# Fourier layer and soft mixture of experts on one core: dummies bridging to the first px, and the combine products as pairs of 64-row products

## The chip, the cores and the metric

The kernel runs on one core of a Trainium2 chip. The metric is the time of one execution in microseconds (us), as the median of several timed runs. One execution was also recorded by the hardware profiler; all durations of single instructions come from that one. The engines are called as in the profile: PE is the matrix engine and PEld its weight load, DVE, ACT and POOL are the vector, scalar and general engines, and SP issues most transfers (DMAs). ACT can issue transfers too, on a queue of its own.

## The reference

Two layers follow each other. The first transforms `x` (8 x 2496 x 256) along the sequence, multiplies by a complex 256 x 256 matrix, adds a bias, shrinks by 0.01 and transforms back. The second is a soft mixture of experts with 8 experts of 4 slots each.

```python
X = np.fft.rfft(x, axis=1)
Yr = Xr @ w_r - Xi @ w_i + b_r
Yi = Xr @ w_i + Xi @ w_r + b_i
Yr = np.sign(Yr) * np.maximum(np.abs(Yr) - lam, 0.0)      # Yi likewise
y = np.fft.irfft(Yr + 1j * Yi, n=x.shape[1], axis=1)
...
logits = x @ phi                         # x: y as 19968 x 256, 32 slots
d = softmax(logits, axis=0)              # over the tokens
slot_out[e] = np.maximum((d.T @ x)[e] @ w1[e], 0.0) @ w2[e]
c = softmax(logits, axis=1)              # over the slots
return c @ slot_out                      # 19968 x 256
```

## The kernel before

The length 2496 is split as 39 x 64, and the transform runs in two stages. Stage a (`a_unit`) multiplies pieces of 117 tokens x 2 groups x 256 columns by the 39-point matrix `f1a`: a product `pa`, which ACT copies from PSUM into a tile `ast`. The `ast` tiles are written to DRAM (`adr`, and for a first part of batch 0 `ad`, `a_write`), and `load_ap` reads them back in another order as `ap`, 512 KB for each of the 40 steps (8 batches x 5 groups of frequencies). Stage f2 multiplies `ap` by the 64-point matrix `smov`: the product `px`. ACT and DVE split `px` into high and low parts (`xth`, `xtl`, `xsm`, `xsh`, `xsl`), `lin_k` and `lin_y` multiply by the weights (`pk`, `py`), and what follows makes logits and slot inputs. The first batch reads `x` through tiles `x0`, later ones through `xr`, of which three buffers exist.

The order of the work is written out by generators with due times: `step_to` puts a generator on a heap, `run_until` takes the earliest, and every engine executes its instructions in the order in which they were recorded. The numbers in `PLAN` are these due times. For the transfers of the beginning the order stands in `PLAN["seq"]`: the token `a0` is the load of `ap` for step 0, `r` the rest of a write of batch 0, `w4` a held write of batch 1, `x8` an `xr` load, `c`, `s` and `k` constants. `keep_warm` issues products of a tile of zeros whose result is not used (`wps`); they are called dummies here.

The first four stage-a pieces of batch 1 (`pa_0` to `pa_6` of that batch, `direct`) are calculated before the first `px`. The write of the piece with groups 4 to 7 is called adr4 below, from its tile `ast_4`; it uses a buffer of the tag `ap` (line 166), so that the third `ap` load can only start when that write has landed.

At the end `slot_out` is known (`po`). It is spread over partitions as high and low parts (`prep`, `rhs`), and the combine loop (line 1183) makes the output: 78 blocks of 128 token pairs, each with two groups of 256 columns. For each block `c_trans` has put transposed combine weights (`pc`, copied to `ct`) into SBUF: rows 0 to 63 belong to the first group, 64 to 127 to the second. `rhs[a]` is 128 x 512 with the slot outputs in rows 0 to 63 of its first half and rows 64 to 127 of its second; the rest is zero. ACT and DVE copy the blocks alternately from PSUM (`pq`, four buffers) to `ost` (nine buffers of 512 KB), and SP writes 512 KB for two blocks. Between the blocks stand the parts for the next batch: `c_prep` splits the combine weights (`chl`, first ACT, then DVE), and `c_trans` transposes them in three pieces. There are 9.75 blocks in a batch.

```python
        mm(
            out=pq,
            lhsT=cts[lo][:, j * TR - lo : j * TR - lo + TR],
            rhs=rhs[a].rearrange("p b d -> p (b d)"),
```

Of the kernel before, what the change touches and what calls it, by code (L numbers as in the profile page):

```python
# [11 lines left out]
F32 = mybir.dt.float32  # L12
# [17 lines left out]
KG = 4  # L30
# [20 lines left out]
def _constants():  # L51
# [95 lines left out]
    "f1": [1.5, 2.15],  # L147
    "kw": [[-40, 9]],
    "ap1": 1.85,
# [8 lines left out]
    "cl_": 'V',  # L158
    "a1": [-50, -49, -48, -47, 3.0, 4.0, 5.9, 6.9, 7.9, 8.9, 10.2],
    "e1": [0, 0, 0, 0, 0, 0, 0, 0, 1, 0, 1],  # L160
# [4 lines left out]
    "lsl": 'PPPPPPPPPPPPPPPPPPPPPPPV',  # L165
    "ast4": {(0, 18): "wr", (1, 0): "wr", (1, 4): "ap"},
    "nd": 4,
    "x1": {(1, 20): 3.5, (2, 0): 7.2},
    "ab1": [[0, 4], [4, 8], [8, 14], [14, 20], [20, 22]],
    "seq": ['a0', 'c', 'a1', 's', 'x8', 'r', 'r', 'r', 'r', 'w4', 'a2', 'x9', 'x10', 'w0', 'k'],  # L170
}
# [12 lines left out]
def fourier_soft_moe_kernel(ctx: ExitStack, tc: tile.TileContext, t: dict, out: bass.AP):  # L184
# [18 lines left out]
    def psum(tag, name):  # L203
        return pp.tile([128, 512], F32, tag=tag, name=name, bufs=psum_bufs[tag])
# [31 lines left out]
    def sp(**kw):  # L236
        tc.keep_in_program_order(nc.sync.dma_start(**kw))
# [16 lines left out]

    def load_x(i):
# [5 lines left out]
        sp(out=xr[:, :ng, :], in_=x[b, :, g : g + ng, :])  # L261
        xrs[(b, g)] = xr
# [63 lines left out]
    def a_unit(b, g, u):  # L326
# [26 lines left out]
        ast = asts[(b, gs[0])]  # L353
        po = psum(("pf", "pl", "pt")[i_ % 3] if first else "pf", f"pa{b}_{g}")
# [6 lines left out]
        yield tu + PLAN['ao']  # L361
        copy(
# [4 lines left out]
        if g + GP == gs[1]:  # L367
            if b == 1 and direct:
                held[gs[0]] = (ad[b], ast, *gs)
                return  # L370
            yield tu + 1.0
            if first:
                a_write(ad0, ast, *gs, 0, R * 4 * KG, q=aq)
                rest.append((ad[b], ast, *gs, R * 4 * KG, QA))
            else:
                a_write(ad[b], ast, *gs)
# [7 lines left out]
    def load_ap(b, grp):  # L384
        ap = wtile([128, KG, D], F32, "ap", f"ap{b}_{grp}")
        src = (ad0 if b == 0 and grp < 2 else ad[b]).rearrange("(k r) g d -> k (r g) d", r=R)
        src = src[grp * 2 * KG : (grp + 1) * 2 * KG, :N2]
        for c in range(2):
            sp(out=ap[c::2], in_=src[c * KG : (c + 1) * KG].rearrange("k n d -> n k d"))
        return ap  # L390

    def f2(s, c, t0):
        yield t0
        b, grp = steps[s]
        ap = aps[s]
        ps = psum("pf", f"px{b}_{grp}_{c}")
        for j in range(KG):
# [47 lines left out]
    def lin_k(s):  # L445
        t0 = 4 * s
        yield t0 + 0.35
        b, g = steps[s]
        pk = psum("pl", f"pk{b}_{g}")
        for c in range(2):  # L450
            lin_s(pk, c, xts[(s, c)])
        yield t0 + PLAN['ko']
        kss[s] = wtile([128, 2, 256], F32, "k1", f"k1{b}_{g}")
        A.copy(out=kss[s], in_=pk.rearrange("p (e x) -> p e x", e=2))

    def lin_y(s, e):
        b, grp = steps[s]
        end = s == ns - 1
        t0 = 4 * s + 1 + (PLAN["T_"]["ye"] if end else 1.35) * e
        yield t0  # L460
        py = psum("pl", f"py{b}_{grp}_{e}")
        lin(py, e, 0, xts[(s, 0)])
        if e == 1 and not end:
            t0 = 4 * s + 3
            yield t0
# [300 lines left out]
    sp(out=wri, in_=t["w"])  # L766
    load_x(7)
    for u, g in enumerate(range(0, G, GP)):
# [314 lines left out]

    rhs = []
    for a in range(2):
        rhs.append(wtile([128, 2, D], F32R, "p_sb", f"rhs{a}"))
        P.memset(rhs[a].bitcast(F32), 0.0)
    slz, hz = pools["slz"], pools["hz"]
# [76 lines left out]
    c_trans(0, 0, V)  # L1165
    for i, tag, dst in ((0, "ps", ((0, A), (1, A))), (1, "pl", ((0, V),)), (1, "pl", ((1, A),))):
        prep = psum(tag, f"prep{i}")
        mm(out=prep[:, :D], lhsT=dmr, rhs=so[i], start=True, stop=True)
        for a, eng in dst:
            r0 = slice(64 * a, 64 * a + 64)  # L1170
            copy(eng, rhs[i][r0, a, :], prep[r0, :D])
    c_trans(0, 4, V)
# [4 lines left out]
    for b in range(B - 1):  # L1177
# [3 lines left out]
        for i0, d, eng in ((0, 4, A), (4, 6, V), (8, 8, A)):  # L1181
            todo.setdefault(at0 + d, []).append((c_trans, b + 1, i0, eng))
    for j in range(NBLK):
        if j % 2 == 0:
            ost = hl_tile(f"ost{j}")
        pq = psum(("pf", "pl")[j % 2], f"pq{j}")
        lo = j * TR - j * TR % F
        for a in range(2):
# [9 lines left out]
        if j < 2 or j >= NBLK - 2:  # L1198
            sp(out=out[j // 2, :, half], in_=ost[:, half])
        elif j % 2:  # L1200
            sp(out=out[j // 2], in_=ost)
        run_until(1000 + 6 * j * TR / CB + 0.1)
        for fn, *args in todo.get(j, []):
            fn(*args)

# [57 lines left out]
```

## Time and profile before

| what | value |
|---|---|
| median of 3 runs | 567.42 us (566.44 to 567.63) |
| the profiled execution, own time | 563.34 us |
| its span in the profile | 561.5 us |
| PE busy | 521.4 us (93% of the span), 4354 matmul records |
| DVE, ACT, POOL busy | 422.0, 298.1, 281.1 us |
| moved by DMA | 121.44 MB, 216 GB/s over the span |
| chain that ended last, by engine | PE 70%, DVE 13%, DMA 10%, ACT 3% |

The profiled execution is 4.08 us shorter than the median of the timed ones. A time in the chain belongs to the instruction that the next one waited for; "idle before <-" names what ended an engine's wait. A product in plain f32 appears as two matmul records, one in fp32r as one. Matmul records overlap, so that the distance from start to start tells what one costs in a row of them.

### The profile page before, as it was taken

The numbers are of one execution on the slowest core, as the hardware profiler recorded it, in microseconds if no ns is written. First come the engines' busy times: TensorE is split into PE (matmuls) and PEld (weight loads), VectorE is DVE, ScalarE is ACT, GpSimd is POOL, SyncE is SP. The second block draws the span as 40 slices with busy tenths as digits, with TensorE's granted clock in tenths as the row PEclk, the third lists the DMA queues.
The fourth block names the chain that finished last, engine by engine and source line by source line (L and its number), as shares of the span: only waits on it lengthen the run. The fifth ranks groups of instructions, "written<-read, shape, count | busy, mean of one in ns | idle before, by whom it ended". The sixth has DMA issues, their size and how long they took to land.

```text
span 561.5 us, 11780 instructions
## 1 busy us (share of the span) xinstructions
PE 521.4 (93%) x4354; PEld 442.2 (79%) x4354; DVE 422.0 (75%) x837; ACT 298.1 (53%) x650; POOL 281.1 (50%) x258
## 2 busy tenths in 40 slices
PE   8669999999999999999999999999899979899794
PEld 4458999989898889889988898987687867367573
DVE  0347897799979897989789978986795764248783
ACT  4435555666566656665665666653433333147572
POOL 0037777766766576658655866684554402000100
PEclk9999999999999999999999999999999998999899
DMA  8788464756476637664757474766634378979898
GB/s 301 249 294 292 151 207 152 210 179 170 163 216 207 189 118 208 207 180 167 204 171 199 155 201 167 222 230 178 186 131 126 113 183 276 392 240 368 325 374 351
DMA packets 93684, 121.44 MB, mean 216 GB/s; under 512 B 46786, under 2 KB 68736, under 8 KB 93628
## 3 DMA queue, kind: packets, MB, share of 16 engines
q1 hardware_dynamic: 93372, 119.63, 65.4%
q10 hardware_dynamic: 256, 1.08, 0.5%
q8 instruction: 34, 0.56, 0.4%
q14 instruction: 22, 0.18, 0.1%
HBM read 69.87 MB, written 50.82 MB: 215 GB/s over the span
## 4 chain that ended last, share of the span: by engine, by line
PE 70%; DVE 13%; DMA 10%; ACT 3%; issue 2%; SPq 1%; ACTq 0%; DVEq 0%
PE py L243 16%; PE px L243 11%; PE pq L243 9%; PE pa L243 8%; PE pk L243 7%; PE pt L532 4%; PE pr L243 3%; DMA eb<-ed 2%; PE pc L1067 2%; DMA ad<-ast 2%; PE pe L243 2%; DMA ap<-adr 2%; DVE mx L180 1%; DVE clpL L180 1%; DVE xtl L180 1%
## 5 line engine op out<-in xcount | busy, mean ns | idle before, releaser
L180 POOL TENSOR_TENSOR rt<-ut,rt 128x512 f32<-128x512 f32 x79 | 111.7, 1414 | 24.4 <-DVE rt L180 18.4
L180 POOL TENSOR_TENSOR xsl<-xsm,xsh 128x256 fp32r<-128x256 f32 x77 | 59.3, 770 | 102.4 <-DVE xsh L180 71.0
L180 POOL TENSOR_TENSOR xl<-xr,xh 117x512 fp32r<-117x512 f32 x73 | 98.5, 1350 | 22.6 <-ACT xh L180 14.7
L243 PE MATMUL px<-smov,ap 128*128 128x128 f32 x640 | 85.6, 277 | 8.0 <-DMA ap<-adr 4.5
L243 PEld LDWEIGHTS px<-smov,ap 128*128 128x128 f32 x640 | 80.3, 193 | 13.7 <-issue 8.1
L180 ACT CAST xth<-px 128x512 fp32r<-128x512 f32 x80 | 46.8, 585 | 73.0 <-PE py L243 37.6
L180 ACT COPY ast<-pa 128x512 f32<-128x512 f32 x86 | 50.3, 587 | 64.5 <-PE pa L243 61.6
L180 DVE SCALAR_TENSOR_TENSOR ut<-py,pk,k 128x256 f32<-128x256 f32 x160 | 69.5, 475 | 15.0 <-PE py L243 13.1
L180 DVE TENSOR_TENSOR xtl<-px,xth 128x512 fp32r<-128x512 f32 x80 | 54.6, 682 | 26.8 <-ACT xsm L180 22.0
L243 PE MATMUL py<-xth,nwsh 128*128 128x256 f32 x160 | 53.5, 334 | 0.0
L180 DVE TENSOR_SCALAR rt<-ut 128x512 f32<-128x512 f32 x69 | 52.2, 756 | 0.5
L243 PE MATMUL pk<-xsh,w_rh 128*128 128x256 f32 x160 | 47.9, 300 | 2.0 <-DVE xsh L180 2.0
L180 ACT COPY T<-pt 128x512 f32<-128x512 f32 x70 | 42.1, 601 | 9.0 <-PE pt L532 7.3
L532 PE MATMUL pt<-pk,rt 128*128 128x128 f32 x320 | 45.9, 273 | 0.9 <-DVE dd L180 0.6
L243 PE MATMUL pk<-xsl,w_rh 128*128 128x256 f32 x160 | 45.1, 282 | 0.0
L243 PE MATMUL pk<-xsh,w_rl 128*128 128x256 f32 x160 | 44.9, 281 | 0.0
L243 PE MATMUL py<-xtl,nwsh 128*128 128x256 f32 x160 | 44.7, 279 | 0.0
L243 PE MATMUL py<-xtl,wdh 128*128 128x256 f32 x160 | 44.7, 279 | 0.0
L243 PE MATMUL py<-xth,wdl 128*128 128x256 f32 x160 | 44.7, 279 | 0.0
L243 PE MATMUL py<-xth,nwsl 128*128 128x256 f32 x160 | 44.7, 279 | 0.0
L243 PE MATMUL py<-xth,wdh 128*128 128x256 f32 x160 | 44.7, 279 | 0.0
L243 PE MATMUL pq<-rhs,ct 128*128 128x512 f32 x156 | 43.1, 415 | 0.3 <-DVE ost L180 0.3
(186 smaller groups left out, 1241.7 us busy)
## 6 DMA issues: line engine op xcount, KB each, us to landing
ap<-adr SPq DMA_DIRECT2D x76, 256.0 KB
out<-ost SPq DMA_DIRECT2D x37, 512.0 KB
xr<-in_x SPq DMA_DIRECT2D x35, 512.0 KB
adr<-ast SPq DMA_DIRECT2D x20, 768.0 KB
w<-in_moe_w SPq DMA_DIRECT2D x25, 512.0 KB
adr<-ast SPq DMA_DIRECT2D x8, 512.0 KB
w<-in_moe_w SPq DMA_DIRECT2D x14, 256.0 KB
x<-in_x SPq DMA_DIRECT2D x11, 256.0 KB
```

The lines of the kernel that those rows point to most:

```text
L180: return lambda *a, **k: self.tc.keep_in_program_order(f(*a, **k))
L243: tc.keep_in_program_order(nc.tensor.matmul(**kw))
L532: tc.keep_in_program_order(nc.tensor.transpose(out=out, in_=in_, identity=identity))
L1067: nc.tensor.transpose(out=pc[:, i * P1 : (i + 1) * P1], in_=chls[b][x][:, 2 * (r + i) : 2 * (r + i) + 2].rearrange("p g h s -> p (g h s)") ...
```

## The change

In the head of the kernel:

- The first `ap` buffers are allocated ahead of everything else, and adr4's tile comes from the three `ast` buffers instead of an `ap` buffer.
- The load of `xr_4` (512 KB) moves from SP, where it stood before the first `ap` load, to ACT's queue behind the last `ad` write.
- In `seq` the rest writes of batch 0 start earlier, and adr4 is no longer in it: it is written when its generator comes, behind the large constants (`k`).
- The dummies before the first `px` go from 9 to 18. `pa_4` and `pa_6` of batch 1, which stood before them, move behind the first `px`, between the parts of step 0.
- In step 0 DVE makes `xtl` last instead of first, and the first half of `py` comes between the two halves of `pk`.

In the combine loop:

- `rhs[a]` is 128 x 256 without zeros, so that POOL's two memsets and two of the four small copies go.
- A step of the loop takes two blocks. For each block and each of the two parts a there are two products of 64 rows and 256 columns, one per group, into two PSUM tiles. Before there was one product of 128 rows and 512 columns.
- ACT copies the first group of both blocks, DVE the second; every output write is 512 KB. `c_prep` and `c_trans` stand behind whole pairs of blocks.

```diff
-    "kw": [[-40, 9]],
+    "kw": [[-40, 18]],
...
-    "a1": [-50, -49, -48, -47, 3.0, 4.0, 5.9, 6.9, 7.9, 8.9, 10.2],
+    "a1": [-50, -49, -1.7, 0.42, 3.0, 4.0, 5.9, 6.9, 7.9, 8.9, 10.2],
...
-    "ast4": {(0, 18): "wr", (1, 0): "wr", (1, 4): "ap"},
+    "ast4": {(0, 18): "wr", (1, 0): "wr"},
...
-    "seq": ['a0', 'c', 'a1', 's', 'x8', 'r', 'r', 'r', 'r', 'w4', 'a2', 'x9', 'x10', 'w0', 'k'],
+    "seq": ['a0', 'r', 'a1', 'c', 's', 'r', 'x8', 'r', 'r', 'a2', 'x9', 'x10', 'w0', 'k'],
...
                 rest.append((ad[b], ast, *gs, R * 4 * KG, QA))
+                if gs[1] == G:
+                    load_x(7, aq)
...
-        V.tensor_tensor(out=xl, in0=pv, in1=xh.bitcast(F32), op=ALU.subtract)
+        if s:
+            V.tensor_tensor(out=xl, in0=pv, in1=xh.bitcast(F32), op=ALU.subtract)
...
+        if not s:
+            V.tensor_tensor(out=xl, in0=pv, in1=xh.bitcast(F32), op=ALU.subtract)
...
-    load_x(7)
+    ap_early = [wtile([128, KG, D], F32, "ap", f"ap0_{grp}") for grp in range(2)]
...
-        pq = psum(("pf", "pl")[j % 2], f"pq{j}")
-        lo = j * TR - j * TR % F
-        for a in range(2):
-            mm(
-                out=pq,
-                lhsT=cts[lo][:, j * TR - lo : j * TR - lo + TR],
-                rhs=rhs[a].rearrange("p b d -> p (b d)"),
-                start=(a == 0),
-                stop=(a == 1),
-            )
-        half = slice(j % 2 * 512, j % 2 * 512 + 512)
-        copy((A, V)[j % 2], ost[:, half], pq)
...
+        pqs = [psum(tag, f"pq{j}_{g}") for g, tag in enumerate(("pf", "pl"))]
+        for k in range(2):
+            c = (j - 1 + k) * TR
+            lo = c - c % F
+            for a in range(2):
+                for g in range(2):
+                    rows = slice(64 * g, 64 * g + 64)
+                    mm(
+                        out=pqs[g][:, k * D : k * D + D],
+                        lhsT=cts[lo][rows, c - lo : c - lo + TR],
+                        rhs=rhs[a][rows],
+                        start=(a == 0),
+                        stop=(a == 1),
+                    )
+        for g in range(2):
+            copy((A, V)[g], ov[:, :, g, :], pqs[g].rearrange("p (k d) -> p k d", d=D))
+        sp(out=out[j // 2], in_=ost)
```

The first place is SP's order in the head, from the last `x` loads to the third `ap` load. `ad` and `adr` are the DRAM tiles of batch 0 (`adr_178` is batch 1), `pk_112` and `smov_110` constants. Before:

```order
L237 DMA xr_4_134<-in_x 128x1024
L237 DMA ap_0_194<-ad_129 64x4x256 x2
L237 DMA pk_112<-in_pk 128x216
L237 DMA ap_1_198<-ad_129 64x4x256 x2
L237 DMA smov_110<-in_smov 128x1088
L237 DMA xr_8_202<-in_x 128x1024
L237 DMA adr_136<-ast_0_137 80x1536
L237 DMA adr_136<-ast_6_147 80x1536
L237 DMA adr_136<-ast_12_158 80x1536
L237 DMA adr_136<-ast_18_169 80x1024
L237 DMA adr_178<-ast_4_186 128x1024
L237 DMA ap_2_209<-adr_136 64x4x256 x2
```

The same stretch of SP's order now:

```order
L239 DMA ap_0_134<-ad_129 64x4x256 x2
L239 DMA adr_136<-ast_0_137 80x1536
L239 DMA ap_1_135<-ad_129 64x4x256 x2
L239 DMA pk_112<-in_pk 128x216
L239 DMA smov_110<-in_smov 128x1088
L239 DMA adr_136<-ast_6_147 80x1536
L239 DMA xr_8_197<-in_x 128x1024
L239 DMA adr_136<-ast_12_158 80x1536
L239 DMA adr_136<-ast_18_169 80x1024
L239 DMA ap_2_201<-adr_136 64x4x256 x2
```

Two transfers of 512 KB have left the stretch: `xr_4` ahead of the first `ap` load, and adr4 (`adr_178<-ast_4`) ahead of the third.

The second place is ACT's order at the same time, from the last `ad` write of batch 0 to the first piece of `px`, as it is now:

```order
L182 COPY ast_18_169<-pa_20_174 128x512
L242 DMA ad_129<-ast_18_169 48x1024
L242 DMA xr_4_178<-in_x 128x1024
L182 COPY ast_0_181<-pa_0_182 128x512
L182 COPY ast_0_181<-pa_2_185 128x512
L182 ACTIVATE nwsh<-wsum 128x512
L182 CAST wdh<-wri 128x512
L182 CAST xth_0_0_256<-px_0_0_243 128x512
```

`xr_4` is issued behind the last `ad` write, and the two copies of `pa_4` and `pa_6`, which stood between `pa_2` and `nwsh`, come after the first pieces of `px`.

The third place is PE's order in the combine loop, behind a piece of transposes (`pc`), where one block was this:

```order
L1067 MATMUL pc_8_7047<-pk_112,chl_1_6916 128x117 x3
L243 MATMUL pq_7052<-rhs_6797,ct_6985 128x512
L243 MATMUL pq_7052<-rhs_6799,ct_6985 128x512
L243 MATMUL pq_7058<-rhs_6797,ct_6985 128x512
L243 MATMUL pq_7058<-rhs_6799,ct_6985 128x512
```

And now (`pq_0` and `pq_1` are the tiles of the two groups):

```order
L1081 MATMUL pc_8_7074<-pk_112,chl_1_6923 128x117 x3
L245 MATMUL pq_0_7080<-rhs_6806,ct_6988 128x256
L245 MATMUL pq_1_7081<-rhs_6806,ct_6988 128x256
L245 MATMUL pq_0_7080<-rhs_6807,ct_6988 128x256
L245 MATMUL pq_1_7081<-rhs_6807,ct_6988 128x256
```

The four products before made two blocks; the four now make one, and the same four names follow once more for the second block of the pair.

More of the change, by code (lines that the diff above doesn't have):

```diff
@@ L165 @@
     "lsl": 'PPPPPPPPPPPPPPPPPPPPPPPV',
-    "ast4": {(0, 18): "wr", (1, 0): "wr", (1, 4): "ap"},
+    "ast4": {(0, 18): "wr", (1, 0): "wr"},
     "nd": 4,
+    "nh": 2,
+    "ao1": {2: 1.2, 3: 0.2},
     "x1": {(1, 20): 3.5, (2, 0): 7.2},
     "ab1": [[0, 4], [4, 8], [8, 14], [14, 20], [20, 22]],
-    "seq": ['a0', 'c', 'a1', 's', 'x8', 'r', 'r', 'r', 'r', 'w4', 'a2', 'x9', 'x10', 'w0', 'k'],
+    "seq": ['a0', 'r', 'a1', 'c', 's', 'r', 'x8', 'r', 'r', 'a2', 'x9', 'x10', 'w0', 'k'],
 }
@@ L253, in split, with load_x @@
         el.tensor_tensor(out=dst_l, in0=src, in1=dst_h.bitcast(F32), op=ALU.subtract)
-    def load_x(i):
+    def load_x(i, q=None):
         if i >= len(xorder) or xorder[i] in xrs:
@@ L260, in load_x @@
         xr = wtile([PX, xc, D], F32, "xr", f"xr{b}_{g}")
-        sp(out=xr[:, :ng, :], in_=x[b, :, g : g + ng, :])
+        (q or sp)(out=xr[:, :ng, :], in_=x[b, :, g : g + ng, :])
         xrs[(b, g)] = xr
@@ L353, in a_unit @@
         ast = asts[(b, gs[0])]
-        po = psum(("pf", "pl", "pt")[i_ % 3] if first else "pf", f"pa{b}_{g}")
+        po = psum(("pf", "pl", "pt")[i_ % 3] if first else "pt" if b == 1 and i_ in PLAN["ao1"] else "pf", f"pa{b}_{g}")
         if direct:
@@ L360, in a_unit @@
             mm(out=po, lhsT=f1l, rhs=xh, start=False, stop=True)
-        yield tu + PLAN['ao']
+        yield tu + (PLAN["ao1"].get(i_, PLAN["ao"]) if b == 1 else PLAN["ao"])
         copy(
@@ L367, in a_unit @@
         if g + GP == gs[1]:
-            if b == 1 and direct:
+            if b == 1 and i_ < PLAN["nh"]:
                 held[gs[0]] = (ad[b], ast, *gs)
@@ L384, in load_ap @@
     def load_ap(b, grp):
-        ap = wtile([128, KG, D], F32, "ap", f"ap{b}_{grp}")
+        ap = ap_early.pop(0) if ap_early else wtile([128, KG, D], F32, "ap", f"ap{b}_{grp}")
         src = (ad0 if b == 0 and grp < 2 else ad[b]).rearrange("(k r) g d -> k (r g) d", r=R)
@@ L451, in lin_k @@
             lin_s(pk, c, xts[(s, c)])
+            if s == 0 and c == 0:
+                yield t0 + 0.45
         yield t0 + PLAN['ko']
@@ L459, in lin_y @@
         t0 = 4 * s + 1 + (PLAN["T_"]["ye"] if end else 1.35) * e
-        yield t0
+        if s == 0 and e == 0:
+            yield t0 - 0.6
+        else:
+            yield t0
         py = psum("pl", f"py{b}_{grp}_{e}")
         lin(py, e, 0, xts[(s, 0)])
+        if s == 0 and e == 0:
+            yield t0
         if e == 1 and not end:
@@ L1082, in fourier_soft_moe_kernel @@
     run_until(TB + 24)
-    rhs = []
-    for a in range(2):
-        rhs.append(wtile([128, 2, D], F32R, "p_sb", f"rhs{a}"))
-        P.memset(rhs[a].bitcast(F32), 0.0)
+    rhs = [wtile([128, D], F32R, "p_sb", f"rhs{a}") for a in range(2)]
     slz, hz = pools["slz"], pools["hz"]
@@ L1165, in fourier_soft_moe_kernel @@
     c_trans(0, 0, V)
-    for i, tag, dst in ((0, "ps", ((0, A), (1, A))), (1, "pl", ((0, V),)), (1, "pl", ((1, A),))):
+    for i, tag, eng in ((0, "ps", A), (1, "pl", V)):
         prep = psum(tag, f"prep{i}")
         mm(out=prep[:, :D], lhsT=dmr, rhs=so[i], start=True, stop=True)
-        for a, eng in dst:
-            r0 = slice(64 * a, 64 * a + 64)
-            copy(eng, rhs[i][r0, a, :], prep[r0, :D])
+        copy(eng, rhs[i], prep[:, :D])
     c_trans(0, 4, V)
@@ L1182, in fourier_soft_moe_kernel @@
             todo.setdefault(at0 + d, []).append((c_trans, b + 1, i0, eng))
-    for j in range(NBLK):
-        if j % 2 == 0:
-            ost = hl_tile(f"ost{j}")
-        pq = psum(("pf", "pl")[j % 2], f"pq{j}")
-        lo = j * TR - j * TR % F
-        for a in range(2):
-            mm(
-                out=pq,
-                lhsT=cts[lo][:, j * TR - lo : j * TR - lo + TR],
-                rhs=rhs[a].rearrange("p b d -> p (b d)"),
-                start=(a == 0),
-                stop=(a == 1),
-            )
-        half = slice(j % 2 * 512, j % 2 * 512 + 512)
-        copy((A, V)[j % 2], ost[:, half], pq)
[L1198 to L1201, printed above, removed]
+    for j in range(1, NBLK, 2):
+        ost = hl_tile(f"ost{j}")
+        ov = ost.rearrange("p (k g d) -> p k g d", g=2, d=D)
+        pqs = [psum(tag, f"pq{j}_{g}") for g, tag in enumerate(("pf", "pl"))]
[15 more added lines that the diff above has]
+        sp(out=out[j // 2], in_=ost)
         run_until(1000 + 6 * j * TR / CB + 0.1)
-        for fn, *args in todo.get(j, []):
-            fn(*args)
+        for i in (j - 1, j):
+            for fn, *args in todo.get(i, []):
+                fn(*args)
 def OUT_SHAPE():
```

## The prediction

> **What bounds the kernel now.** The chain of waits for the whole span is 70% PE, so I looked for the stretches in which PE isn't what ends last. The windows of the engines show two: the first 40 us, and the combine loop from 501 us on. The change touches these alone.
>
> For the head I read the chain in order of time, PE's timeline, SP's waits and the windows of single microseconds (columns of the last: length; busy of PE, PEld, DVE, ACT, POOL; granted PE clock, DMA share, GB/s).
>
> ```profile
> 15.74 3.19 DMA ad<-ast
> ...
> 18.98 0.69 SPq L237
> ...
> 35.53 4.01 DMA ap<-adr
> ```
>
> ```profile
> 35.69 0.28 PE L243 MATMUL py<-xtl,wdh 128*128 128x256 f32 x1
> 39.68 1.72 PE L243 MATMUL px<-smov,ap 128*128 128x128 f32 x8 [3.71 <-DMA ap<-adr]
> ```
>
> ```profile
> SPq L237 <- DMA adr<-ast: 6.9, 3, 5.0
> ```
>
> ```profile
> 17.00:18.00 1.00, 0.16 (x1) 0.19 (x2) 1.00 (x2) 0.16 (x1) 0.00 (x0) 1.00 0.87 256
> 18.00:19.00 1.00, 1.00 (x3) 0.49 (x3) 0.95 (x2) 0.03 (x1) 0.00 (x0) 1.00 0.09 33
> ...
> 47.00:48.00 1.00, 0.72 (x6) 0.73 (x7) 0.97 (x4) 0.22 (x1) 1.00 (x2) 1.00 0.00 0
> ```
>
> ```profile
> 40.00:45.00 5.00, 5.00 (x29) 4.71 (x28) 0.00 (x0) 2.44 (x5) 1.27 (x1) 0.66 1.00 350
> ```
>
> PE has done its last `py` of step 0 at 35.97 and waits 3.71 us for the third `ap` load. SP couldn't issue that load before 34.89, since it waited up to 5.0 us for the `adr` writes; the load itself took 4.01 us. After the wait the granted clock is 0.66 in the mean of 5 us, which costs 5 x 0.34 = 1.7 us. So the head ends when the writes of batch 0 have landed. Whatever PE does earlier has a slack of 3.7 us.
>
> For the combine loop I read the same columns in four stretches, the end of the DMAs and SP's timeline:
>
> ```profile
> 503.00:512.00 9.00, 8.38 (x48) 6.64 (x47) 6.64 (x12) 6.71 (x13) 0.00 (x0) 1.00 0.79 313
> 512.00:524.00 12.00, 10.01 (x50) 7.40 (x48) 10.10 (x18) 7.98 (x17) 2.75 (x2) 1.00 1.00 399
> 524.00:536.00 12.00, 10.39 (x47) 8.06 (x48) 9.62 (x17) 6.36 (x15) 1.38 (x1) 0.86 0.68 275
> 536.00:554.00 18.00, 17.07 (x87) 13.28 (x85) 14.06 (x26) 12.74 (x25) 0.00 (x0) 1.00 1.02 405
> ```
>
> ```profile
> 554.00:557.00 3.00, 0.00 (x0) 0.00 (x0) 0.28 (x1) 0.00 (x0) 0.00 (x0) 1.00 1.03 407
> ```
>
> ```profile
> 559.00:560.00 1.00, 0.00 (x0) 0.00 (x0) 0.00 (x0) 0.00 (x0) 0.00 (x0) 0.50 0.72 279
> ```
>
> ```profile
> 502.83 54.74 SPq L237 DMA_DIRECT2D out<-ost  x41
> ```
>
> PE is done before 554, and the transfers run on at 407 GB/s until about 559.7: the output writes end last, and PE's time counts only where it leaves them without work. At 407 GB/s the output of 39 x 0.524 = 20.45 MB needs 50.2 us. What is missing to that rate, in GB/s by us, is (407 - 313) x 9 + 8 x 12 + (407 - 275) x 12 + 2 x 18 = 2.56 MB, or 6.3 us. PE is nearly full there and waits for little but `chl`; the longest of these waits:
>
> ```profile
> 524.41 0.71 PE L1067 MATMUL pc<-pk,chl 117*128 117x117 f32 x4 [1.88 <-DVE chl L180]
> ```
>
> **The head, part by part.** (1) `xr_4`, 512 KB, no longer stands before the first `ap` load. The DMAs are busy until 18 us (share 0.87 in the row 17 to 18, 0.09 in the next), so 0.524 MB at about 0.4 MB/us is 1.3 us of traffic beside the last `ad` write, which takes 3.19 us and lands at 18.93. That write can hardly be issued earlier: its data come from PE's last product of batch 0. Its 192 KB need 0.5 us at that rate, and the smallest load, at the start (64 KB), took 1.85 us from issue to first use:
>
> ```profile
> 0.74 0.39 SPq L237 DMA_DIRECT2D f1a<-in_f1a  x1
> ```
>
> ```profile
> 2.59 0.23 DVE L180 CAST f1h<-f1a 117x128 fp32r<-117x128 f32 x1 [1.20 <-DMA f1a<-in_f1a]
> ```
>
> So it lands earlier by 0 to 1.3 us; I take 0.8, since most of the rest is latency. Behind that write `xr_4` finds the DMAs idle, since the first `ap` load waits for the same write. ACT's extra issue (0.3 us, as the other writes on its queue) delays only copies whose readers come later.
>
> (2) adr4, 512 KB, no longer stands before the third `ap` load:
>
> ```profile
> 28.00:34.00 6.00, 5.29 (x42) 4.74 (x40) 2.78 (x7) 2.79 (x6) 1.57 (x2) 1.00 1.02 387
> ```
>
> The DMAs are full, so 0.524 / 0.387 = 1.35 us go, all of it if nothing else holds the load. adr4 now stands behind `pk1`; its reader is step 5, at some 80 us. It delays the fourth `ap` load by 1.35 us, but between 47 and 48 us the DMAs move nothing, so that load has landed by 47, and `px` of step 3 starts at 52.45: hidden.
>
> ```profile
> 52.45 1.06 PE L243 MATMUL px<-smov,ap 128*128 128x128 f32 x8
> ```
>
> (3) PE's timeline has the old dummies and the first `px`:
>
> ```profile
> 19.23 2.63 PE L243 MATMUL wps<-warm 128*128 128x512 f32 x9
> 23.53 2.02 PE L243 MATMUL px<-smov,ap 128*128 128x128 f32 x16 [1.67 <-DMA pk<-in_pk]
> ```
>
> The nine more dummies (9 cost 2.63 us before), the moves of `pa_4` and `pa_6`, DVE's order in step 0 and the split of `pk` and `py` I cost at nothing. The wait for the third load covers them: with that load 2.15 us earlier, `px` of step 2 starts at 37.5, still 1.6 us behind the old end of `py`. The moves themselves shorten the way from first `px` to `py`, as `xtl` leaves the way to `pk`; that only lengthens the wait. The dummies start behind `pa_2`, which ends at 14.65 + 1.88 = 16.5 (row below), and end at about 16.5 + 18 x 0.29 = 21.7, ahead of the first `px` (23.5 - 0.8 = 22.7); without that cover they would cost their excess.
>
> The new wait of ACT for the first `adr` write (it frees the tile for `pa_4`) has the loads of step 1 and the copies for step 0 behind it. The write stands right after the first `ap` load, so it lands some 1.2 us after it, while `px` alone takes 2.0 us: no cost.
>
> Head: 0.8 + 1.35 = 2.15 us, from 1.0 (the first term nothing, the second cut short) to 2.65. Everything behind is shifted with it, since PE is nearly full in the middle:
>
> ```profile
> 200.00:300.00 100.00, 98.31 (x886) 88.63 (x885) 87.09 (x172) 61.85 (x137) 67.04 (x59) 1.00 0.59 180
> ```
>
> **The combine loop.** Before, two blocks cost four products of 512 columns:
>
> ```profile
> 504.43 0.94 PE pq L243 x4
> 505.37 0.40 PE pc L1067 x4
> ```
>
> Now they are eight of 256 columns, half as high. The price of one such product isn't in the trace. From above it is bounded by products of 256 columns on the whole array, one after another, 1.42 / 12 = 0.118 us:
>
> ```profile
> 53.50 1.42 PE pk L243 x12
> ```
>
> Eight make 0.94 us, so nothing is won. From below it is two at a time, 0.47 us. What does show packing are products on quarters of the columns, against the same width on the whole array:
>
> ```profile
> 483.90 5.36 PE L243 MATMUL hps<-w,z 128*32 128x512 f32 x48
> ```
>
> ```profile
> 14.65 1.88 PE L243 MATMUL pa<-xr,f1a 117*128 117x512 f32 x4
> ```
>
> 0.47 us each on the whole array, 0.11 packed: four run nearly at once. I take the lower end, with a little loss, 0.5 us a pair of blocks, because this is the nearest row in kind. What it doesn't show is packing by rows, and its weights are 32 columns wide:
>
> ```profile
> L243 PEld LDWEIGHTS pq<-rhs,ct 128*128 128x128 f32 x156 | 28.3, 195 | 6.0 <-DVE ost L180 1.1
> ```
>
> ```profile
> L243 PEld LDWEIGHTS po<-w,z 128*32 128x32 f32 x128 | 4.0, 110 | 3.1 <-issue 0.6
> ```
>
> 96 columns more cost 85 ns, so 128 columns cost about 0.113 us. There are twice as many loads now, each with 128 columns; if loads of the two halves can't run beside each other, they alone fill 0.9 us. The Trainium skill ("TensorE: Matmul & The Clock Gate", section on LDWEIGHTS) speaks against the change here: a load costs its columns over 1.2, in ns, whatever its rows, an estimate of 107 ns, which agrees with the 113. "TensorEngine Tiling (Array Packing)", Key Properties, says that different tiles can load weights and multiply in parallel; no run here shows it for rows. By the first alone the loop would gain nothing, by the second what I take.
>
> The chain of waits gives the steps around `chl`:
>
> ```profile
> 507.98 0.59 ACT ost L180
> 508.56 0.53 ACT chl L180
> ...
> 515.74 0.70 DVE chl L180
> ...
> 522.36 1.91 DVE chl L180
> ...
> 531.79 1.50 DVE chl L180
> ...
> 553.58 0.69 DVE ost L180
> ```
>
> With 0.5 us, PE needs 4.875 x 0.5 + 1.1 (11 `pc` at 0.10) = 3.5 us for a batch, plus one wait for `chl`: a copy, ACT's and DVE's part (0.59 + 0.53 + 0.70, the chain's first rows above) less the one pair between, 1.3 us. The writes need 4.875 x 0.524 / 0.407 = 6.3 us. ACT and DVE make as many copies as before and were busy 71% and 78% at the full rate (12.74 and 14.06 of 18 us). So the writes bound the loop from its start. Batch 0 has no `c_prep`, so its pairs follow at about a DVE copy each (0.69 us) against 1.29 us for a write, and the lead of some 3 us covers the two long `chl` steps of DVE (1.91 and 1.50 us against 0.70). Of the 6.3 us about 0.9 stay at the start, where the first write is not issued earlier than at 502.8, and 0.6 I leave for gaps: 4.8 us go, from 3.0 to 5.4. The three copies less of `rhs` and memsets I cost at nothing: DVE's `ct` holds the first product as well.
>
> **The sum.** 563.34 - 2.15 - 4.8 = 556.4 us for the profiled execution. It was 4.08 us shorter than the median; I carry the difference over unchanged: 567.42 - 6.95 = **560.5 us**.
>
> **The rivals.**
>
> *The products don't pair.* For it: the weight loads. Then a pair of blocks stays at 0.94 us, and only one pair instead of three blocks stands between `c_prep` and the first `pc`, which adds about 0.6 us of waiting in each of six batches: products end 3.6 us later. From the last product (553.6, where DVE's last copy starts) to the end (559.7) are 6.1 us, of which a last copy and write need 4; so 2.1 us are swallowed and the loop is 1.5 us longer: 567.42 - 2.15 + 1.5 = 566.8.
>
> *Slower: each product shows its weight load.* After an idle stretch products of this size start 0.23 us apart:
>
> ```profile
> 26.99 0.39 PE L243 MATMUL pk<-xsh,w_rh 128*128 128x256 f32 x1 [1.44 <-DVE xsh L180]
> 27.22 0.28 PE L243 MATMUL pk<-xsh,w_rl 128*128 128x256 f32 x1
> ```
>
> If changing the rows at each product has this price, a pair costs 1.84 us, the products end 39 x 0.9 = 35 us later and the kernel takes 567.42 - 2.15 + 35 - 2.1 = 598. It decides from the point where the products end 4.2 us later, 0.11 a pair, or 0.13 us a product. Against it: full-array products hide their loads, at 0.118.
>
> *The head gives nothing*, because the third load is then held by something else (the issue on SP, a slow read): 567.42 - 4.8 = 562.6. Against it: the wait is for exactly the writes that have less traffic ahead.
>
> *The clock stays.* The wait before `px` of step 2 goes from 3.7 to about 3.4 us (37.5 less an end of `py` some 1.8 us earlier). If that isn't long enough to halve the clock, 1.7 us more go: 558.8. In the trace 1.67 us of idling at 22 us kept the clock and 1.88 us at 522 lost it (0.86 in the row 524 to 536), so I give it little. By the Trainium skill ("TensorE: Matmul & The Clock Gate", Part 1) the clock halves after an idle window of about 3.4 us that runs freely; the 1.88 us don't agree with it.
>
> **How the numbers follow.** Forecast 60%, clock 10%, head nothing 9%, no pairing 14%, loads shown 7%. The range goes from 557.0 (both terms at their best, 567.42 - 2.65 - 5.4, the clock's 1.7 and the runs' spread of 0.6 on top) to 566.5 (just below no pairing). A measurement tells some 0.2% (1.1 us, so 566.3) from no change. No pairing lies on that border: I split it 5, 6, 3. Faster 0.84, same 0.06, slower 0.10.
>
> **What would show it.** The last `ad` write lands near 18.1, the third `ap` load is issued near 32.7, and `px` of step 2 starts near 37.5 after a wait of 3 us or more. In the loop four `pq` records take some 0.24 us, PE's busy share falls, the DMAs are full from 506 on, and they end about 4.8 us earlier counted from the first output write. Wrong would be a pair of 0.9 us, or DMA gaps that stay in 524 to 536, or an SP issue of the third load that doesn't move.

## The result, and the profile after

The changed kernel takes 572.11 us (median of 12 runs) against 566.55 us for the kernel before (12 runs). The ratio of the runs is 1.0121, with a 95% interval from 1.0090 to 1.0151: it is slower by 1.2%, 5.6 us above the median of before, where the prediction had 7 us gained. The profiled execution after took 572.88 us, with a span of 571.0 us.

**The head.** The chain of waits of the changed kernel (start, us, what was waited for), and SP's timeline behind it:

```profile
16.33 2.70 DMA ad<-ast
...
26.39 8.38 DMA adr<-ast
...
35.54 4.32 DMA ap<-adr
```

```profile
19.09 1.39 SPq L239 DMA_DIRECT2D ap<-ad  x2
...
34.91 1.25 SPq L239 DMA_DIRECT2D ap<-adr  x2
```

The last `ad` write lands at 19.03 (before 18.93), and the third `ap` load is issued at 34.91 (before 34.89). In this pair of executions nothing has moved. PE's timeline:

```profile
16.83 4.67 PE L245 MATMUL wps<-warm 128*128 128x512 f32 x18
...
40.10 2.05 PE L245 MATMUL px<-smov,ap 128*128 128x128 f32 x8 [3.07 <-DMA ap<-adr]
```

`px` of step 2 starts at 40.10, not at 37.5, behind a wait of 3.07 us. The 18 dummies don't bridge to the first `px` either: they end near 21.5, and PE waits 2.04 us for the first `ap` load. Two windows of the changed kernel, and the row of the kernel before for the second:

```profile
40.00:45.00 5.00, 4.90 (x20) 4.64 (x21) 0.00 (x0) 1.97 (x4) 1.27 (x1) 0.50 0.98 351
24.00:29.00 5.00, 5.00 (x27) 3.97 (x26) 3.26 (x8) 2.31 (x5) 0.00 (x0) 0.66 0.89 256
```

```profile
24.00:29.00 5.00, 3.04 (x22) 2.48 (x21) 3.28 (x8) 1.72 (x4) 0.00 (x0) 1.00 0.91 296
```

The clock is lost a first time right behind the first `px`, and for longer behind the third load (0.50, where the kernel before has 0.66). How much of the first 60 us runs at half clock varies, though: 3.4 to 13.7 us in the nine executions with the old head below (mean 7.6), 6.8 to 13.7 in the seven with the new one (mean 10.2). So the new head does not keep the clock better; that it keeps it worse is not clear of the spread.

**The middle.** Between some 50 us and the combine loop the change alters no PE instruction and no transfer. Yet most of the 9.5 us between the two profiled spans arises there. 5.1 us of them lie ahead of the last batch's `gd` write, which starts at 453.97 before and at 459.05 after. In the stretches 384 to 392 and 408 to 416 us the granted clock is 0.79 after and 1.00 before, which makes 3.4 us. I don't put these 5.1 us down to the change: in the nine executions with nine dummies below, old head and new, this write starts anywhere from 454.0 to 460.5, and the one that I predicted from is the earliest of all.

The last chain of waits before the loop differs as well. In the last batch the data go through DRAM twice, as `gd` and as `ed`, which is read back as `eb`; behind `eb` come the products `pd` and `pr`, and then the first ones with the experts' weights, `hps`. First the chain's lines of before, then of after:

```profile
474.59 3.66 DMA eb<-ed
...
478.39 0.79 PE pd L243 x2
...
479.75 1.50 PE pr L243 x24
```

```profile
479.69 5.83 DMA eb<-ed
...
485.66 2.47 PE pd L245 x4
488.13 1.81 PE pr L245 x24
```

The last `eb` load takes 5.83 us in place of 3.66, and the products behind it run slowly. The windows of that stretch in the changed kernel (columns as in the prediction; third from the end is the granted clock) show why:

```profile
485.00:490.00 5.00, 4.34 (x29) 2.08 (x30) 0.98 (x2) 0.30 (x1) 0.00 (x0) 0.66 1.02 390
```

0.34 x 5 = 1.7 us of clock are lost there. From the start of this load to the first `hps` it takes 12.90 us in place of 9.31; of the 3.6 us more, the load has 2.2 and what stands behind it 1.4.

**The combine loop.** A pair of blocks does cost less. At full clock the chain mostly has eight `pq` products, which make a pair, at 0.67 to 0.72 us; the four of before cost 0.94:

```profile
512.50 0.55 PE pc L1081 x4
513.05 0.67 PE pq L245 x8
```

But PE's waits for `chl` have grown, and the DMAs still have gaps. PE's timeline and the windows of the loop in the changed kernel:

```profile
518.65 0.62 PE L1081 MATMUL pc<-pk,chl 117*128 117x117 f32 x4 [2.12 <-DVE chl L182]
...
533.40 0.62 PE L1081 MATMUL pc<-pk,chl 117*128 117x117 f32 x4 [1.25 <-DVE chl L182]
...
541.52 0.62 PE L1081 MATMUL pc<-pk,chl 117*128 117x117 f32 x4 [2.42 <-DVE chl L182]
```

```profile
512.00:519.00 7.00, 4.88 (x54) 3.83 (x52) 4.70 (x10) 5.20 (x11) 0.00 (x0) 1.00 0.93 369
519.00:527.00 8.00, 7.22 (x51) 5.60 (x49) 5.73 (x12) 4.57 (x9) 1.37 (x1) 0.57 0.82 331
527.00:543.00 16.00, 11.67 (x117) 9.04 (x118) 14.17 (x23) 10.17 (x24) 3.07 (x2) 1.00 0.91 363
543.00:547.00 4.00, 4.00 (x32) 3.18 (x30) 2.53 (x5) 2.12 (x5) 0.00 (x0) 0.57 0.90 363
```

Behind each of the two long waits (2.12 and 2.42 us) the granted clock is 0.57 in the mean, and the DMAs move 331 to 369 GB/s in these four stretches, not 407. From the first output write to the end are 571.0 - 511.77 = 59.2 us; before they were 561.5 - 502.83 = 58.7.

So there are three questions. Is the head's new order at fault? Why is the `eb` load slower, in code that was not changed? And where does the loop's cheaper product go?

### The profile page after: what moved, and what is told of

It reads as the page before. It is cut to its first block, busy times and chain, and to the rows that moved or that the text cites. A ratio compares the mean times of both kernels' runs of the same rounds, so it can differ in the third digit from the quotient of the medians.

```text
span 571.0 us, 12094 instructions
## 1 busy us (share of the span) xinstructions
PE 524.4 (92%) x4518; PEld 445.6 (78%) x4518; DVE 423.2 (74%) x837; ACT 296.9 (52%) x648; POOL 280.6 (49%) x256
## 4 chain that ended last, share of the span: by engine, by line
PE 71%; DVE 13%; DMA 8%; ACT 3%; issue 3%; SPq 1%; ACTq 0%; DVEq 0%
PE py L245 15%; PE px L245 10%; PE pa L245 9%; PE pq L245 7%; PE pk L245 7%; PE pt L546 4%; PE pr L245 3%; PE pc L1081 2%; DMA eb<-ed 2%; DMA gp<-gd 2%; PE pe L245 2%; DMA adr<-ast 1%; DVE mx L182 1%; DVE clpL L182 1%; DVE clpd L182 1%
## 5 line engine op out<-in xcount | busy, mean ns | idle before, releaser
L245 PE MATMUL px<-smov,ap 128*128 128x128 f32 x640 | 87.5, 282 | 6.9 <-DMA ap<-adr 3.1
L245 PEld LDWEIGHTS px<-smov,ap 128*128 128x128 f32 x640 | 82.3, 197 | 12.5 <-issue 6.8
L245 PE MATMUL pk<-xsh,w_rh 128*128 128x256 f32 x160 | 49.7, 310 | 0.0
L546 PEld LDWEIGHTS pt<-pk,rt 128*128 128x128 f32 x320 | 36.5, 140 | 5.2 <-ACT T L182 1.1
```

What stands on the lines that cost most here:

```text
L245: tc.keep_in_program_order(nc.tensor.matmul(**kw))
L546: tc.keep_in_program_order(nc.tensor.transpose(out=out, in_=in_, identity=identity))
```

## The experiments

Each ratio is to runs of the kernel before on the same chip, with its 95% interval. "The loop" is the time from the first output write to the end, in the profiled execution.

**Head alone, loop alone, and two forms of the loop.** e1 has the new head and the old loop, e2 the old head and the new loop.

> The new head with the old combine loop. Theory A (the head is where the time is lost, by itself and through half-clock stretches that its shift sets off at 386 and 410 us): the k copy of step 2 comes about 1.4 us later than in the kernel before, the combine loop starts 4 to 9 us later than there, and the time is 1.008 to 1.012 of before. Theory B (the head costs its own 1.4 us and the stretches in the middle are chance): 1.0025, and the clock of its runs is as before but for the one stretch more at 24 to 29 us. Theory C (the loss is the combine loop's): 0.997 to 1.0025.

> The old head with the new combine loop. Theory A: the head and the middle are as before, and the loop by itself is within 1 us of the old one (60.8 against 60.0 us from the first product to the end in the two profiles): 0.999 to 1.003. Theory C: 1.008 to 1.012, with the loop 5 to 7 us longer than before. If the prediction's term for the loop held without the late start: 0.991 to 0.995.

e3 is e2 with this edit:

```diff
-            todo.setdefault(at0 + 1, []).append((c_prep, b + 1))
+            todo.setdefault(at0 - 1, []).append((c_prep, b + 1))
```

> As e2_comb_only, with the split of the combine weights (chl) issued one pair of blocks earlier, so that a pair of blocks stands between it and the transposes that read it. Theory: the loop's gain is given back by PE's waits for chl (2.1, 0.8, 1.3, 2.4 us in the changed kernel) and the half-clock stretches behind them. Then these waits go below 0.5 us, the DMAs run at some 400 GB/s from the first batch on, the loop ends 3 to 5 us earlier than in e2_comb_only, and the time is 0.992 to 0.996 of before. Rival: the copies of ACT and DVE or the DMAs themselves hold the loop; then the waits move to pq's buffers and the time is within 1 us of e2_comb_only.

e4 is e2 with this one:

```diff
-            for a in range(2):
-                for g in range(2):
+            for g in range(2):
+                for a in range(2):
```

> As e2_comb_only, with the two products of one group of columns recorded one after the other, so that consecutive products stand in the same 64 rows twice and then in the other 64. If products of different rows run beside each other and those of the same rows don't, a pair of blocks costs about 0.8 to 0.95 us in place of 0.6 and PE's products end about 39 x 0.25 = 10 us later, or 3 to 8 us with the writes' slack: 1.005 to 1.014. If the pairing isn't what makes 0.6 us, a pair costs 0.6 us again and the time is that of e2_comb_only.

| run | median, us | ratio to before | loop, us |
|---|---|---|---|
| e1, head only | 571.72 | 1.0102 (1.0070 to 1.0134) | 59.7 |
| e2, loop only | 569.61 | 1.0059 (1.0022 to 1.0096) | 62.6 |
| e3, loop, earlier split | 565.64 | 0.9987 (0.9955 to 1.0018) | 56.2 |
| e4, loop, products unpaired | 569.37 | 1.0063 (1.0032 to 1.0095) | 63.7 |

Both parts lose by themselves. e1's time is in the range of theory A, but not for A's reason, as the next runs show; e2's lies between the ranges of both theories. For the loop, e3 bears out the waits: with the split earlier the longest wait for `chl` is 0.91 us, the loop gets 6.4 us shorter in the profile, and 0.7% of the time goes. It misses the forecast 0.992 to 0.996 all the same. e4 has 0.74 us for eight products in its timeline, as e2 has, and not 0.8 to 0.95: the order of the products makes no difference. (e4's 63.7 us come from the longest of its 12 runs, 575.01 us.)

The head's loss was not where I looked. The third `ap` load of e1 is issued at 36.32, but three executions with the old head have it at 36.83 (e4), 36.70 (e2) and 35.77 (e3): the head itself varies that much, and the profile that I predicted from (34.89) was one of the fastest. What the four old-head executions share against the two with the new head is the `eb` load: 3.63 to 3.92 us against 4.65 and 5.83. And the DMA view has something else in those stretches. For the changed kernel between 481 and 482, inside the load:

```profile
q1 hardware_dynamic: 1211, 0.15, 97.2%
q8 instruction: 1, 0.02, 6.0%
```

For the kernel before the same row stands between 482 and 483, some four us after the load has landed:

```profile
q1 hardware_dynamic: 114, 0.41, 99.4%
q8 instruction: 1, 0.02, 6.4%
```

It is one transfer of 16 KB. 6.0% of 16 engines for one us are 0.96 us of one engine, by which the packets behind it on that engine may be late (an estimate; no run shows it). The page of the changed kernel counts 36 of them, and 4518 products with as many weight loads, which makes 251 PE instructions for each:

```profile
PE 524.4 (92%) x4518; PEld 445.6 (78%) x4518; DVE 423.2 (74%) x837; ACT 296.9 (52%) x648; POOL 280.6 (49%) x256
...
q8 instruction: 36, 0.59, 0.4%
```

The Trainium skill ("Runtime: NRT & Kernel Launch", section "Instruction fetch mechanics") says that an engine's code is fetched while it runs, in blocks of 16 KiB or 256 instructions over a DMA queue of its own; the 251 agree. So the nine added dummies, 9 products and 9 weight loads, may have moved the place of a fetch some 440 us later.

**Dummies alone.** e5 is the kernel before with 18 dummies, e6 the new head with 9 (and the old loop). The edit of e5, and that of e6 the other way round:

```diff
-    "kw": [[-40, 9]],
+    "kw": [[-40, 18]],
```

e9 is e5 with dummies of half the width, so that 18 take the time of nine:

```diff
-            mm(out=ps, lhsT=warm[:, 0:128], rhs=warm, start=True, stop=True)
+            mm(out=ps[:, :256], lhsT=warm[:, 0:128], rhs=warm[:, :256], start=True, stop=True)
```

> The kernel before with 18 dummies in the head in place of 9, and nothing else. In the two executions with the new head a transfer of 16 KB on the queue called instruction falls 2.0 us after the first issue of the last eb load, which then takes 4.65 and 5.83 us, and the clock halves right behind it; in the four with the old head it falls 7.6 to 8.2 us after that issue, and the load takes 3.63 to 3.92 us. Theory F (the fetches of PE's instructions move with the count of PE instructions ahead of them, and this one now meets the eb load): the 9 dummies alone bring it to about 2 us after the issue, the load takes 4.5 us or more, a half-clock stretch follows it, the way from its issue to the first hps is 2.5 to 4 us longer than the 9.3 us of before, and the time is 1.003 to 1.010 of before. Theory H (the loss of the new head comes from its moved loads and copies): the load takes 3.6 to 3.9 us and the time is 0.998 to 1.002.

> As e1_head_only with 9 dummies in place of 18. Theory F: the fetch is again some 7 to 8 us behind the issue of the last eb load, the load takes 3.6 to 3.9 us, no half-clock stretch follows it, and the time falls from e1_head_only's 1.010 to 1.001 to 1.006. Theory H: the time stays at 1.007 to 1.013.

> As e5_before_18_dummies, with dummies of 256 columns in place of 512: 18 of them take the time of the old nine (about 2.6 us), and PE has nine products more ahead of everything that follows, as in e5. Theory F (the place of the instruction fetches): the fetch again falls 2 to 3 us behind the issue of the last eb load, the way from the gd write to the first hps takes 31 to 34 us in place of 28 to 30.5, and the time is 1.006 to 1.012. Rival D (the longer dummies themselves cost, by what PE does in the head): the time is 0.998 to 1.003, as with nine dummies.

e5 gave 571.22 us, 1.0094 (1.0065 to 1.0124). e6 gave 566.61 us, 1.0006 (0.9978 to 1.0035). e9 gave 570.69 us, 1.0085 (1.0049 to 1.0121). So the new head with nine dummies costs nothing that can be measured, and nine more dummies cost 0.9% with the old head and the new one, whether they take PE's time or not. That the number of the dummies does it is shown. That it works through the fetch fits less well: e5's own profile has the fetch inside the load, but a load of only 4.38 us, no half-clock stretch behind it, and 10.0 us from the load's start to the first `hps` against the 9.3 of before, where 2.5 to 4 us more were expected. The chain of e9, whose head and loop are those of before, has all of it:

```profile
476.38 4.91 DMA eb<-ed
481.29 0.14 issue
481.42 2.32 PE pd L243 x4
483.75 2.06 PE pr L243 x24
```

**The loop's waits, filled.** e7 is e2 with dummies where PE waits:

```diff
+        if b > 1 and i0 == 0:
+            dummy(6)
         pc = psum("pt", f"pc{b}_{i0}")
```

> As e2_comb_only, with six dummies (products of the 128-column identity with itself, about 0.22 us each at full clock) ahead of the first transposes of each of six batches, where PE waits for chl. Theory A for the loop (the waits cost twice, since the half-clock stretches behind them slow the products that follow): the half-clock stretches of 3.4, 1.7 and 3.4 us in the loop go or shrink to one of 1.7, the loop from first write to end takes 58 to 60 us in place of 62.6, and the time falls from 1.006 to 0.998 to 1.003. Rival (the waits themselves are the cost, the clock follows): the loop stays at 62 to 64 us, since the dummies take PE's time where it would be waiting or beyond, and the time is 1.005 to 1.010.

e7 took 564.28 us, 0.9966 (0.9933 to 0.9998), and its loop 56.4 us. Its windows, for the same stretches as above, and behind them a row of e2:

```profile
512.00:519.00 7.00, 6.20 (x62) 5.06 (x63) 5.61 (x13) 4.93 (x11) 1.38 (x1) 1.00 0.94 373
519.00:527.00 8.00, 7.76 (x80) 6.57 (x77) 6.59 (x12) 6.04 (x14) 0.40 (x1) 1.00 0.95 378
527.00:543.00 16.00, 14.45 (x143) 11.82 (x141) 13.52 (x23) 10.00 (x22) 2.68 (x2) 1.00 0.96 381
```

```profile
531.00:546.00 15.00, 12.28 (x84) 9.58 (x82) 10.15 (x18) 7.40 (x16) 1.37 (x1) 0.66 0.71 285
```

Work without use makes the kernel 0.9% faster than e2: the clock is 1.00 in all three stretches, and the DMAs move 373 to 381 GB/s. The rival would have kept the loop at 62 to 64 us. So it is the half-clock products behind the waits, more than the waits themselves, that cost the time.

A long wait does not always lose the clock. In the old loop the third wait for `chl` is 1.9 us in all six executions. Behind it the clock halves in three (before, e1, e9) and stays in three (e5, e6, e12), here in e12:

```profile
525.59 0.59 PE L1067 MATMUL pc<-pk,chl 117*128 117x117 f32 x4 [1.88 <-DVE chl L180]
```

```profile
524.00:536.00 12.00, 9.22 (x51) 7.05 (x51) 11.09 (x19) 6.94 (x16) 2.27 (x2) 1.00 0.82 327
```

In the new loop without filling or earlier split (after, e2, e4, e11, e13) nine waits of 2.1 us or more were met at full clock. Eight went with a half-clock stretch, and one of 2.12 us in e13 did not. What decides it I don't know.

**The price of a product.** e8 is e2 with three kinds of products in the three thirds of the loop:

```diff
-                    rows = slice(64 * g, 64 * g + 64)
+                    rows = slice(0, 64) if j < 26 else slice(64 * g, 64 * g + 64) if j < 52 else slice(0, 128)
```

> As e2_comb_only, but the products of the first 13 pairs of blocks all use rows 0 to 63, those of the next 13 alternate as in the changed kernel, and those of the last 13 use all 128 rows with 256 columns (so the first and last parts of the output are other sums than the reference's). Eight products in a row without transposes take 0.60 us in the changed kernel. If they are that cheap because products of different rows run beside each other, the first part takes 0.9 to 1.0 us for eight, and the last part 0.94. If rows have nothing to do with it, the first part takes 0.60 as well; if 64 rows are cheaper than 128 by themselves, the first part takes 0.60 and the last 0.94.

Two thirds of e8's products are not those of the changed kernel, so its output is another one and its time (586.71 us, one run) says nothing; only the prices are read. PE's timeline at full clock, for 16 products always in the same rows and for 40 on all rows (both of e8), and for 16 that alternate (e2):

```profile
517.93 2.17 PE L243 MATMUL pq<-rhs,ct 64*128 64x256 f32 x16
...
571.89 5.21 PE L243 MATMUL pq<-rhs,ct 128*128 128x256 f32 x40
```

```profile
511.14 1.21 PE L243 MATMUL pq<-rhs,ct 64*128 64x256 f32 x16
```

That is 0.136, 0.130 and 0.076 us a product. Products of different rows do run beside each other: eight cost 0.60 us, not 1.04 to 1.09. In e4 they overlap as well, though each pair of neighbours there has the same rows half of the time; why the order makes no difference I did not try. The transposes pay for it: `pc` of four takes 0.55 us from its start to that of the next product behind 64-row products (512.98 - 512.43 in the changed kernel). In the kernel before it is 504.19 - 503.87 = 0.32 us, and between the full-height products of e8 564.19 - 563.86 = 0.33 us:

```profile
503.87 0.56 PE L1067 MATMUL pc<-pk,chl 117*128 117x117 f32 x4
504.19 1.17 PE L243 MATMUL pq<-rhs,ct 128*128 128x512 f32 x4
```

```profile
563.86 0.56 PE L1067 MATMUL pc<-pk,chl 117*128 117x117 f32 x4
564.19 1.20 PE L243 MATMUL pq<-rhs,ct 128*128 128x256 f32 x8
```

The Trainium skill ("TensorEngine Tiling (Array Packing)", Key Properties) says that a change of the tiling mode drains the engine; the 0.22 us more agree with it.

**Together.** e10 is the changed kernel with 9 dummies in the head (`"kw": [[-40, 9]]`), e3's edit, and three dummies at e7's place (`dummy(3)`). e11 is the changed kernel with 9 dummies and nothing else.

> The changed kernel with 9 dummies in the head, the split of the combine weights one pair of blocks earlier, and three dummies ahead of the first transposes of each of six batches. If the three findings add up (9 dummies: 1.0006 for the head; the loop without half-clock stretches and waits: e7_comb_filled's 0.997 or some 1 to 2 us less), the time is 0.992 to 0.998 of before, with no half-clock stretch in the loop and 55 to 57 us from first write to end. If filling and the earlier split are in each other's way (PE is then too full for the writes): 0.998 to 1.004.

> The changed kernel with 9 dummies in place of 18. If its loss of 1.2% is the sum of the fetch's new place (1.0102 and 1.0006 for the new head with 18 and with 9 dummies) and the new loop (1.0059 alone), the time is 1.003 to 1.009 and the eb load takes 3.6 to 3.9 us. If the new head and the new loop act on each other, it stays at 1.010 to 1.014.

e10 took 566.53 us, 1.0007 (0.9972 to 1.0042), although its profiled execution was short, with a loop of 55.0 us; its runs fell into 561 to 563 and 566 to 569 us. e11 took 571.30 us in 6 runs, 1.0108 (1.0064 to 1.0152). Both miss what the sum of the parts gave and fall into the ranges of their rivals. In e11's profile the transfer of 16 KB stood inside the `eb` load again, which took 5.16 us. Nine dummies looked like a border, so the next three have two: e12 is the kernel before, e13 the changed kernel and e14 is e10, each with this line:

```diff
+    "kw": [[-40, 2]],
```

> The kernel before with 2 dummies in the head in place of 9. Theory F (a border): PE now has 7 products and their weight loads less ahead, the fetch falls 7 us or more behind the issue of the last eb load in every execution, the load takes 3.6 to 4.0 us; the executions of before that had the fetch inside the load are gone, and the time is 0.993 to 0.999 of before. Rival (the dummies are needed for the clock in the head, and the fetch is no matter): px of step 0 runs at half clock, and the time is 1.000 to 1.005.

> The changed kernel with 2 dummies. Theory F (a border): the fetch is behind the load, and what is left is the new loop's loss, 1.002 to 1.007. Rival (the new head and the new loop lose together, whatever the fetch does): 1.009 to 1.014.

> As e10_new_head_9_filled_early with 2 dummies in the head. Its runs with 9 fell into two groups, 561 to 563 and 566 to 569 us, against a median of 565.5 for before. Theory F (a border): with the fetch kept out the upper group goes, and the time is 0.988 to 0.996 of before. Rival (the two groups come from something else): two groups again, and 0.998 to 1.004.

e12 took 565.16 us, 0.9972 (0.9943 to 1.0001). e13 took 569.06 us, 1.0044 (1.0016 to 1.0072). e14 took 563.99 us, 0.9952 (0.9924 to 0.9979), in one group from 560 to 567 us: it is faster than the kernel before by 0.5%. So e10's split and filling were not in each other's way; both loops take 55 us. e12's interval still holds no change. e14's windows, with the DMAs nearly full from 512 us on:

```profile
512.00:524.00 12.00, 11.29 (x116) 9.12 (x115) 10.41 (x21) 8.85 (x21) 1.37 (x1) 1.00 1.01 397
524.00:536.00 12.00, 9.74 (x95) 7.52 (x92) 10.69 (x20) 8.22 (x19) 3.00 (x2) 1.00 0.99 394
```

All 16 profiled executions, by their dummies. The third column gives the microsecond in which the 16 KB transfer starts (the beginning of it), counted from the first issue of the last `eb` load:

| dummies | executions | 16 KB transfer, us | `eb` load, us | from the `gd` write to the first `hps`, us |
|---|---|---|---|---|
| 2 | e12, e13, e14 | 7.3 to 8.3 | 3.83 to 4.09 | 28.1 to 28.8 |
| 9 | before, e2, e3, e4, e6, e7, e10 | 7.4 to 8.1 | 3.63 to 4.00 | 28.3 to 30.4 |
| 9 | e8, e11 | 2.3 to 3.0 | 5.16 to 5.44 | 29.9 to 32.9 |
| 18 | after, e1, e5, e9 | 1.3 to 2.3 | 4.38 to 5.83 | 31.1 to 33.5 |

No execution with the transfer inside the load has a load of under 4.3 us, and none with it behind has one over 4.1. The fetch before it shows the same. With 18 dummies it starts 1.3 to 1.6 us behind the start of the `gd` write, which then takes 3.55 to 3.91 us; with nine 2.3 to 3.1 us and with two 4.0 to 4.3, and the write takes 2.67 to 3.24. All this goes together in 16 executions, which is not yet a cause: no edit moved a fetch by other means than the dummies. Why the same code has it at two places with nine dummies stays open. So does a part of the 0.9%: the last column has some 3 of 5 us. From the first `hps` to the first output write nothing differs (18.9 us in before, e1, e5, e6, e9 and e12). The old loop takes 57.6 us in the mean of before, e6 and e12 and 59.4 in that of e1, e5 and e9; these 1.8 us were not followed.

## Why the prediction was wrong, point by point

**What bounds the head: right, with a bad base.** In all 16 executions PE's wait before `px` of step 2 is ended by the third `ap` load. But I took times to 0.1 us from one execution. In nine with the old head that load is issued at 34.5 to 36.9 (mean 35.8), in seven with the new head at 33.9 to 36.3 (mean 34.8).

**Term 1, `xr_4` out of the way, 0.8 us: right.** The first `ap` load is issued at 19.4 in the mean of the nine and at 18.7 in that of the seven, 0.7 us earlier. The profiled pair (18.98, 19.09) does not show it, and no run moves `xr_4` alone.

**Term 2, adr4 out of the way, 1.35 us: failed.** From the issue of the first `ap` load to that of the third are 16.4 us in the mean of the old head and 16.2 in that of the new. I wrote that "behind that write `xr_4` finds the DMAs idle". It doesn't. The DMA view between the two issues, before (18.98 to 34.89) and after (19.09 to 34.91):

```profile
q1 hardware_dynamic: 2023, 4.49, 83.9%
```

```profile
q1 hardware_dynamic: 1904, 4.04, 76.1%
q10 hardware_dynamic: 95, 0.32, 5.2%
```

q10 is ACT's queue: 0.32 MB of `xr_4` run there after the first `ap` load is issued. The 512 KB that leave the stretch are replaced by most of the 512 KB that were moved behind the write; 0.13 MB remain, 0.45 us at the rate of 282 GB/s. I had looked at what the moved load waits for, and not at when its bytes flow.

**Step 3, the dummies at nothing: this is the step that failed most.** I hid their duration behind the wait of 3.7 us, and that cover holds: e9's short dummies cost as much as e5's long ones. What they cost is their number: 0.9%, some 5 us, against the 2.15 us that the whole head was to gain. About 3 of the 5 us go with the new places of two instruction fetches; the rest stays open, and that the fetches are the cause is argued, not shown. "Everything behind is shifted with it" was the wrong sentence: the fetches move against the work.

**Pairs at 0.5 us: right in kind, mis-sized.** 0.60 us, 0.67 with transposes between, and 0.22 us more for each group of transposes: 0.55 + 0.55 + 0.45 = 1.55 us a batch, where I had 1.1. At full clock PE would need some 4.7 us a batch (three pairs at 0.67, 1.875 at 0.60, and 1.55), not 3.5; with 1.2 us of waiting that leaves 0.4 us under the 6.3 of the writes, not 1.5.

**One wait of 1.3 us for `chl` a batch, covered by a lead of 3 us: failed.** The waits of the changed kernel are 2.12, 0.78, 1.25, 2.42, 0.41 and 0.41 us, 1.2 in the mean where I had 1.3; that is luck, since the single ones differ sixfold. And I carried PE's price at full clock through them. The waits of before were shorter (0.62, 0.52, 1.88, 0.88, 0.24 and 0.23 us). Behind the long ones of the new loop the clock is mostly halved, the lead is gone, and the writes don't bound the loop: it takes 61.1 us in the mean of after, e2, e11 and e13, and 58.5 in the mean of the six executions with the old loop. What I used against the clock in the head ("1.88 us at 522 lost it") stood in my own text and I did not apply it to the loop that I made emptier; as a rule it was too firm as well, since waits of that length keep the clock in half of the cases. e7 and e14 come near what I predicted for the loop, once the clock is held: e14's loop is 58.7 - 55.1 = 3.6 us shorter than that of before, against my 4.8.

**The rivals.** "The products don't pair" is refuted by e8. "Slower because each product shows its weight load" had the sign, with a mechanism that is wrong. "The head gives nothing" was right in time (e6), by luck: it named the issue on SP or a slow read, but what took adr4's place is `xr_4`'s traffic, and the load is still issued 0.9 us earlier in the mean. "The clock stays" was a rival for the head only, where it should have been one for the loop, with the opposite sign.

**The sum.** The parts alone give +0.9% (dummies), +0.6% (loop) and nothing (head), 1.5% together, against 1.2% measured; the intervals overlap. With two dummies the changed kernel is at 1.0044; against the kernel before with two (e12, 0.9972) that makes 1.007, near the loop's 0.6%.

## What to carry to other kernels

When an edit makes PE quicker inside a loop that something else bounds, look for what PE will then wait for, and also price the products behind each wait of 2 us or more at half the clock (here it came with eight of nine); filling the wait, or issuing its cause earlier, may be worth more than the edit. An instruction added far ahead is not free because its time is hidden: nine of them cost 0.9% here. It moves the fetches of its engine's code, and one of them can land in a transfer that others wait for; the DMA view shows where they stand. Before a term of a few us is read from one profile, see how far a second execution of the same code differs there.

## What was not expected of the hardware

A single 16 KB transfer of PE's code inside the `eb` load went with 0.5 to 2 us more for that load, and in four of six such executions with 1.7 us or more of lost clock behind it. The Trainium skill, at the place named above, has the crossing of such a block as mostly hidden; here a load of 3.63 to 4.09 us without the transfer took 4.38 to 5.83 with it. Six useless products at each of six places made e2 faster by 0.9%. And in nine executions of the old head the issue of the third `ap` load varied by 2.4 us (34.5 to 36.9).
